# V's loads of the last twenty pairs: 38 rows a band in one, all 144 groups in 3 KB rows in the other

## The chip, the cores and the metric

The kernel runs on one core of a Trainium2 chip. The metric is the device time of one execution in microseconds (us). Engines are named as in the profile: PE (TensorE), DVE (VectorE), ACT (ScalarE), POOL (GpSimd), SP (SyncE); PEld is TensorE's weight load. SP computes nothing here: it issues nearly all transfers, in program order, and stands still at an issue until what that transfer needs is done.

## The reference

Attention in two parts over 8 batches x 8 heads of 576 tokens x 64, then a gated feed-forward layer over all 4,608 tokens.

```python
q_d = q.reshape(B, H, Sd, 4, D).mean(axis=3)      # k_d, v_d the same: 144 groups of four
out_d = sm_attn(q_d, k_d, v_d)                     # full attention over 144 groups
out_up = np.repeat(out_d, 4, axis=2)
mask = np.abs(pos[:, None] - pos[None, :]) < 4     # each token sees 7 neighbours
out_local = softmax(where(mask, scale * q @ k.T, -1e9)) @ v
x = (out_up + out_local)                           # to [B*S, H*D]
out = (np.maximum(x @ w_gate, 0) * (x @ w_val)) @ w_out
```

## The kernel before

**Pairs and slots.** Two heads of a batch make a pair; there are 32. The work is written out by hand, one `slot(n)` after another (L635), for n from -2 to 33; within a slot each engine's instructions have the order in which the code lists them, and a pair passes through several slots. For the last twenty pairs (`p >= NPE`, that is p >= 12) the steps are: loads of Q and K (L161) five or six slots ahead, the loads of V (`load_v` L186, `load_v4` L215) four slots ahead, the casts to 16 bits three and two slots ahead, the DMA transpose of Q and K (`turn_qk` L262) two ahead, the group sums of Q and K on POOL (`pool_qk` L316) one ahead, scores and softmax in the pair's own slot, the DMA transposes of the weights (`turn_a` L487) one after, and the output matmuls (`outputs` L511) and `add_x` two after. The first twelve pairs use TensorE in place of those transposes.

**SP's order in a slot** for these pairs: `turn_a(n-1)` (transposes of `en` and `ad`), `turn_qk(n+2)` (two transposes), the loads of Q and K, `load_v(n+4)` (two loads), `load_v4(n+4)` (one load), then the stores of finished output rows.

**V comes twice.** `load_v` brings overlapping windows of 32 tokens for the local attention: two bands of 48 partitions (0 to 47 and 64 to 111) of `vst`, 18 windows each. A row of a window is one packet of 64 floats, 256 B. The local matmul (L518) reads rows 0 to 37 of a band. `load_v4` brings the first 128 of the 144 groups of each head, four tokens (1 KB) a row, one group a partition; POOL adds the four tokens in two steps (`sum_v4` L221) into `s4`. The last 16 groups come from `v16` by four small matmuls (L377, `v_ps`), with `pool_sb` as weights. `copy_vd` (L418) puts both into `vd`.

**The coarse weights.** `weights_d` (L468) multiplies the exponentials `ed` [80, 4, 144] by the reciprocal sums on POOL into `ad`: 128 keys in blocks 0 to 3, and 16 keys of each in block 4. The transpose then gives `adt` with five blocks of 80, and L535 multiplies them with `vd`: four matmuls over 128 rows, four over 64.

**Feed-forward.** `ffn_do` emits pieces of the feed-forward layer on TensorE between the attention steps, four or five a slot in the slots of the last twenty pairs. What is left when all pairs are through runs at the end.

Of the kernel before, what the change touches and what calls it, by code (L numbers as in the profile page):

```python
# [10 lines left out]
FP32 = mybir.dt.float32  # L11
FP16 = mybir.dt.float16
AF = mybir.ActivationFunctionType
ALU = mybir.AluOpType
# [3 lines left out]
VR = 112  # L18
# [23 lines left out]
def _dap(t_ap: bass.AP, extra_off: int, dims) -> bass.AP:  # L42
    return bass.AP(tensor=t_ap.tensor, offset=t_ap.offset + extra_off, ap=list(dims))
# [3 lines left out]
def kernel(  # L47
# [10 lines left out]
    nc = tc.nc  # L58
    B, H, S, D = q.shape
# [10 lines left out]
    NW = S // 32  # L70
    NPE = 12
# [16 lines left out]
    def pool(name, bufs):  # L88
        return ctx.enter_context(tc.tile_pool(name=name, bufs=bufs))
# [3 lines left out]
    NQK, NA, NV = 4, 2, 3  # L93
    cpool = pool("kept", 1)
    qk_t = [cpool.tile([128, KW], FP16, name=f"qkT{i}") for i in range(NQK)]
    v_t = [cpool.tile([VR, NW, D], FP32, name=f"vst{i}") for i in range(NV)]
    en_t = [cpool.tile([96, 12, 64], FP16, name=f"en{i}") for i in range(NA)]
    ad_t = [cpool.tile([80, 6, 128], FP16, name=f"adn{i}")[:, 0:5] for i in range(NA)]
    p_nat = pool("nat", 4)
    p_v4 = pool("v4", 3)  # L100
    p_16 = pool("h16", 3)
    p_at = pool("at", 2)
    p_adt = pool("adt", 2)
# [15 lines left out]
    p_t1 = pool("t1", 1)  # L119
    p_qkd = pool("qkd", 2)  # L120
    p_sm = pool("sm", 1)
    p_e = pool("e", 2)
    p_st = pool("st", 4)
    p_ed = pool("ed", 2)
    p_vd = pool("vd", 4)
    p_s4 = pool("s4", 3)
    p_od = pool("od", 2)
    psum = ctx.enter_context(tc.tile_pool(name="psum", bufs=6, space=bass.MemoryType.PSUM))
    psum_d = ctx.enter_context(tc.tile_pool(name="psum_d", bufs=2, space=bass.MemoryType.PSUM))

# [5 lines left out]
        nc.gpsimd.memset(t[:, KO + S :], 0.0)  # L136
    for t in en_t + ad_t:
        nc.vector.memset(t, 0.0)

    def bank(shape, name, dt=FP32):  # L140
        return psum.tile(shape, dt, name=name, tag="bank")
# [17 lines left out]
    st = {}  # L159
# [26 lines left out]
    def load_v(p):  # L186
        off = 2 * p * S * D
        vst = v_t[p % NV]

        def win(rows, lo, par, w, nw):  # L190
            nc.sync.dma_start(
                vst[64 * par + lo : 64 * par + lo + rows, w : w + nw, :],
                _dap(
                    v,
                    off + (32 * (2 * w + par) - 3 + lo) * D,
                    [[D, rows], [64 * D, nw], [1, D]],
                ),
            )


        if p == 0:
            win(48, 0, 0, 1, NW - 1)
            win(45, 3, 0, 0, 1)
        else:
            win(48, 0, 0, 0, NW)
        if p == NP - 1:
            win(48, 0, 1, 0, NW - 1)
            nc.vector.memset(vst[96:VR, NW - 1, :], 0.0)
            win(35, 0, 1, NW - 1, 1)
        else:  # L210
            win(48, 0, 1, 0, NW)
        st[p]["vst"] = vst


    def load_v4(p):  # L215
        st[p]["v4"] = v4 = p_v4.tile([128, 2, 4 * D], FP32, name="v4", tag="v4")
        nc.sync.dma_start(
            v4, _dap(v, 2 * p * S * D, [[4 * D, 128], [S * D, 2], [1, 4 * D]])
        )

    def sum_v4(p):  # L221
        s = st[p]
        v4 = s.pop("v4")
        s2 = v4[:, :, 0 : 2 * D]
        nc.gpsimd.tensor_tensor(out=s2, in0=s2, in1=v4[:, :, 2 * D : 4 * D], op=ALU.add)
        s["s4"] = p_s4.tile([128, 2, D], FP32, name="s4", tag="s4")
        nc.gpsimd.tensor_tensor(
            out=s["s4"], in0=s2[:, :, 0:D], in1=s2[:, :, D : 2 * D], op=ALU.add
        )
# [129 lines left out]
                )  # L359

    def pool_v(p):
        s = st[p]
        v16 = s["v16"]
        s["vp"] = vp = bank([128, 4, D], "v_ps")
        v2 = v16.rearrange("p (h l) d -> p h l d", h=2)

        for l in range(8) if p < NPE else ():
            nc.tensor.matmul(
                out=vp[:, 0:2, :],
                lhsT=pool_sb[:, 128 - 16 * l : 256 - 16 * l],  # L370
                rhs=v2[:, :, l, :],
                start=(l == 0),
                stop=(l == 7),
            )
        for c in range(2):
            for h in range(2):
                nc.tensor.matmul(  # L377
                    out=vp[64 * h : 64 * h + 64, 2 + c, :],
                    lhsT=pool_sb[:, 128 - 32 * c : 192 - 32 * c],
                    rhs=v2[:, h, 8, :],  # L380
                    start=True,
                    stop=True,
                )
# [34 lines left out]
    def copy_vd(p):  # L418
        s = st[p]
        s["vd"] = p_vd.tile([128, 4, D], FP16, name="vd", tag="vd")  # L420
        vp = s.pop("vp")
        if p < NPE:
            nc.scalar.copy(out=s["vd"], in_=vp)
        else:
            nc.scalar.copy(out=s["vd"][:, 2:4], in_=vp[:, 2:4])
            nc.scalar.activation(
                out=s["vd"][:, 0:2], in_=s.pop("s4"), func=AF.Copy, scale=0.25
            )

    def exp_d(p, h):  # L430
# [37 lines left out]
    def weights_d(p):  # L468
        s = st[p]
        rd = p_st.tile([80, 4], FP32, name="rd", tag="rd")  # L470
        nc.vector.reciprocal(out=rd, in_=s.pop("sd"))
        ad = s["ad"] = ad_t[p % NA]
        ed = s.pop("ed")
        for o, i, n in (
            (ad[:, 0:4], ed[:, :, 0:128], 128),
            (ad[:, 4].rearrange("p (i t) -> p i t", i=4)[:, :, 0:16], ed[:, :, 128:144], 16),
        ):
            nc.gpsimd.tensor_tensor(  # L478
                out=o, in0=i, in1=rd[:, :, None].to_broadcast([80, 4, n]), op=ALU.mult
            )  # L480

    def adt_tile(p):
        t = p_adt.tile([128, 512], FP16, name="adt", tag="adt")
        st[p]["adt"] = t[:, 0:400].rearrange("p (a b) -> p a b", b=80)
        return st[p]["adt"]

    def turn_a(p):  # L487
# [23 lines left out]
    def outputs(p):  # L511
        s = st[p]
        at, adt, vd, v16 = s["at"], s["adt"], s["vd"], s["v16"]
        s["up"] = up = [bank([128, 9, 32], "u_ps") for _ in range(2)]
        for l in range(9):
            for par in range(2):
                for h in range(2):
                    nc.tensor.matmul(  # L518
                        out=up[par][64 * h : 64 * h + 64, l, :],
                        lhsT=v16[64 * par : 64 * par + 38, 9 * h + l, :],  # L520
                        rhs=at[
                            64 * par : 64 * par + 38,
                            3 * h + l // 3,
                            32 * (l % 3) : 32 * (l % 3) + 32,
                        ],
                        start=True,
                        stop=True,
                    )
        op = bank([128, S // 4], "o_ps")
        for tail in range(2):  # L530
            for c in range(2):
                lo, n, skip = (0, 80, 0) if c == 0 else (80, 64, 16)
                for h in range(2):
                    rows = slice(64 * h, 64 * h + 64) if tail else slice(0, 128)
                    nc.tensor.matmul(  # L535
                        out=op[64 * h : 64 * h + 64, lo : lo + n],
                        lhsT=vd[rows, 2 + c if tail else h, :],
                        rhs=adt[rows, 4 if tail else 2 * h + c, skip : skip + n],
                        start=(tail == 0 and c == 0),
                        stop=(tail == 1 and c == 1),  # L540
                    )
        s["od"] = p_od.tile([128, S // 4], FP32, name="od", tag="od")
        nc.scalar.copy(out=s["od"], in_=op)  # L543
# [91 lines left out]
    def slot(n):  # L635
# [3 lines left out]
        while loaded[0] < min(NP, n + (5 if n < NPE - 2 else 6)):  # L639
            load(loaded[0])  # L640
            if loaded[0] < NPE:
                load_v(loaded[0])
            loaded[0] += 1
        at_stage(n + 4, load_v, load_v4, pe=False)
        store_y()
        at_stage(n, scores, scores_d)
        at_stage(n - 1, turn_en_pe, pe=True)
        at_stage(n, pool_v, mask_l, shift_l, copy_vd, exp_l, max_d)
        if n == 0:
            cast_qk_act(1)  # L650
# [10 lines left out]
        at_stage(n - 1, turn_ad_pe, pe=True)  # L661
        at_stage(n, lambda p: exp_d(p, 0))
        at_stage(n - 1, outputs, pe=True)
        at_stage(n - 2, outputs, pe=False)
        at_stage(n, sums, weights_l)
        at_stage(n - 1, x_stage, pe=True)
# [6 lines left out]
        if n + 2 >= NPP:  # L673
            at_stage(n + 2, cast_v, pe=True)
        at_stage(n + 1, pool_qk, pe=True)
        at_stage(n, weights_d)
        at_stage(n + 3, cast_qk_act, cast_qk_pool, pe=False)
        at_stage(n + 2, cast_v, sum_v4, pe=False)
        if 1 <= n < 5:
            load_h_weights(n - 1)  # L680
# [45 lines left out]
```

## Time and profile before

| | us |
|---|---|
| median of 3 runs | 408.92 |
| lowest and highest | 406.75, 412.8 |
| profiled execution | 405.34 |
| its span, first to last instruction | 403.5 |
| PE busy in the span | 375.6 |
| DVE, ACT, POOL busy | 253.2, 210.4, 191.5 |

Matmuls are pipelined and their ends are modelled, so a busy PE is not a PE at its peak; the start of one group to the start of the next is the better measure. In 117.76 to 273.58 us (slots 13 to 27) POOL is busy for 93.36 of 155.82 us and DVE for 112.11. POOL's instructions of that stage, per pair (line, tile, shapes, count, busy us and mean ns; from the groups kept apart by shape):

```profile
L478 POOL TENSOR_TENSOR adn<-ed,rd 80x512 f16<-80x512 f16 x16 | 16.6, 1037 | 37.4 <-ACT h L247 19.2 <-DVE rd L471 11.0 <-ACT r L576 7.2
...
L225 POOL TENSOR_TENSOR v<-v 128x256 f32<-128x256 f32 x16 | 11.6, 723 | 0.0
...
L227 POOL TENSOR_TENSOR s<-v 128x128 f32<-128x128 f32 x16 | 7.3, 454 | 1.3
L478 POOL TENSOR_TENSOR adn<-ed,rd 80x64 f16<-80x64 f16 x16 | 4.6, 290 | 0.0
```

The last numbers of a line are the idle time of the engine before these instructions and what ended it.

### The profile page before, as it was taken

What the parts mean: (1) busy time and instruction counts of PE and PEld (TensorE: products, weight loads), DVE (VectorE), ACT (ScalarE), POOL (GpSimd) and SP (SyncE); (2) the same over time, 40 slices, a digit from 0 to 9 for tenths busy, and PEclk for the clock granted to TensorE, in tenths of its full rate; (3) what the DMA queues carried; (4) which work ended last, traced back from release to release, by engine and by line L of the source; (5) the groups of instructions that cost most, each with busy time, mean ns of one, the idle gap of its engine ahead of it and who ended that gap; (6) DMA issues with size and microseconds to landing.
All of it is one profiled execution on the core that took longest, in us unless ns stands there. A gap on an engine that the chain in (4) does not pass through costs nothing.

```text
span 403.5 us, 11622 instructions
## 1 busy us (share of the span) xinstructions
PE 375.6 (93%) x4544; PEld 196.4 (49%) x4544; DVE 253.2 (63%) x639; ACT 210.4 (52%) x600; POOL 191.5 (47%) x252
## 2 busy tenths in 40 slices
PE   2699998898999999999999998999699999999996
PEld 2587555454544444444445444444244444444442
DVE  2798699887878767675767675777557432222220
ACT  3577678775757545564545555555345322332321
POOL 5587778764778666666555565544551100000000
PEclk9999999999999999999999999999899999999999
DMA  7999999998999999999999899898831100100012
GB/s 192 229 210 224 232 231 211 233 177 200 213 221 203 178 178 203 204 192 193 198 213 200 191 191 197 184 165 182 168 108 53 51 28 26 54 26 28 37 41 105
DMA packets 172700, 64.24 MB, mean 159 GB/s; under 512 B 150166, under 2 KB 168038, under 8 KB 172646
## 3 DMA queue, kind: packets, MB, share of 16 engines
q1 hardware_dynamic: 166470, 58.63, 69.8%
q0 software_dynamic: 5824, 4.72, 7.7%
q8 instruction: 35, 0.57, 0.6%
q10 hardware_dynamic: 352, 0.16, 0.2%
q14 instruction: 19, 0.16, 0.1%
HBM read 47.87 MB, written 9.44 MB: 142 GB/s over the span
## 4 chain that ended last, share of the span: by engine, by line
PE 77%; ACT 7%; DVE 6%; DMA 4%; issue 3%; POOL 2%; SPq 1%; ACTq 0%; POOLq 0%
PE h_ps L568 42%; PE y_ps L584 23%; PE o_ps L535 2%; PE s_ps L336 2%; ACT ed L437 2%; PE u_ps L518 2%; PE d_ps L353 2%; DVE sm L411 2%; DMA nat<-in_k_dram 1%; PE t_ps L283 1%; DVE s_ps L388 1%; DVE mx L410 1%; PE t_ps L304 1%; PE v_ps L377 1%; ACT r L576 1%
## 5 line engine op out<-in xcount | busy, mean ns | idle before, releaser
L578 DVE TENSOR_TENSOR g<-r,h_ps 128x512 f16<-128x512 f16 x108 | 73.9, 684 | 97.2 <-PE h_ps L568 88.2
L568 PE MATMUL h_ps<-xT,wg_sb 128*128 128x512 f16 x432 | 113.1, 384 | 3.0 <-DVE xT L552 3.0
L568 PE MATMUL h_ps<-xT,wv_sb 128*128 128x512 f16 x432 | 112.4, 383 | 0.0
L584 PE MATMUL y_ps<-wo_sb,g 128*128 128x512 f16 x432 | 98.6, 379 | 0.0
L576 ACT ACTIVATE r<-h_ps 128x512 f16<-128x512 f32 x108 | 64.4, 596 | 46.9 <-PE h_ps L568 46.4
L478 POOL TENSOR_TENSOR adn<-ed,rd 80x512 f16<-80x512 f16 x64 | 41.2, 663 | 67.1 <-ACT r L576 22.8
L568 PEld LDWEIGHTS <-wv_sb 128*128 128x128 f16 x432 | 42.6, 99 | 55.4 <-issue 5.5
L584 PEld LDWEIGHTS <-g 128*128 128x128 f16 x432 | 41.6, 98 | 49.2
L568 PEld LDWEIGHTS <-wg_sb 128*128 128x128 f16 x432 | 38.9, 99 | 43.6 <-issue 1.9
L592 ACT COPY y_sb<-y_ps 128x512 f32<-128x512 f32 x36 | 21.1, 586 | 68.9 <-PE y_ps L584 57.6
L323 POOL TENSOR_TENSOR t<-qkT 128x576 f32<-128x576 f16 x27 | 30.9, 1145 | 39.6 <-DMA qkT<-h 32.7
L437 ACT ACTIVATE ed<-d_ps,nb 80x144 f16<-80x144 f32 x128 | 47.6, 383 | 0.0
L260 POOL CAST v<-vst 112x1152 f16<-112x1152 f32 x32 | 36.7, 1147 | 8.3 <-DMA vst<-in_v_dram 5.3
L449 ACT ACTIVATE e<-sm 96x456 f16<-96x456 f32 x32 | 18.6, 583 | 35.9 <-DVE sm L411 35.8
L249 POOL CAST h<-nat 96x768 f16<-96x768 f32 x35 | 29.7, 849 | 5.6 <-DMA nat<-in_k_dram 3.0
L388 DVE TENSOR_TENSOR s_ps<-s_ps,mask_sb 96x228 f32<-96x228 f32 x64 | 22.2, 390 | 16.0 <-PE s_ps L336 14.0
L552 DVE TENSOR_TENSOR xT<-u_ps,od 128x288 f16<-128x288 f32 x64 | 26.0, 446 | 5.0 <-ACT od L543 5.0
L394 DVE TENSOR_REDUCE d_ps<-d_ps 80x2 f32<-80x288 f32 x64 | 28.9, 452 | 0.0
L247 ACT CAST h<-nat 96x768 f16<-96x768 f32 x29 | 24.3, 841 | 4.3 <-DMA nat<-in_k_dram 4.3
L411 DVE TENSOR_TENSOR sm<-s_ps,mx 96x228 f32<-96x228 f32 x64 | 25.1, 392 | 2.2
L437 ACT ACTIVATION_READ_ACCUMULATOR ed<-d_ps,nb 80x1 f32 x128 | 26.4, 206 | 0.0
L461 DVE TENSOR_TENSOR en<-e,rl 96x456 f16<-96x456 f16 x32 | 23.9, 747 | 1.1
(54 smaller groups left out, 363.5 us busy)
## 6 DMA issues: line engine op xcount, KB each, us to landing
vst<-in_v_dram SPq DMA_DIRECT2D x62, 216.0 KB, 5.2
out_dram<-y_sb SPq DMA_DIRECT2D x36, 256.0 KB, 3.4
nat<-in_q_dram SPq DMA_DIRECT2D x20, 288.0 KB, 3.5
nat<-in_k_dram SPq DMA_DIRECT2D x20, 288.0 KB, 4.3
v<-in_v_dram SPq DMA_DIRECT2D x20, 256.0 KB, 4.8
nat<-in_q_dram SPq DMA_DIRECT2D x12, 192.0 KB, 7.8
nat<-in_k_dram SPq DMA_DIRECT2D x12, 192.0 KB, 5.3
wg_sb<-in_moe_w_gate_dram POOLq DMA_DIRECT2D x4, 384.0 KB, 8.4
```

What stands on the lines that cost most here:

```text
L249: nc.gpsimd.tensor_copy(out=dst, in_=src)
L260: nc.gpsimd.tensor_copy(out=s["v16"], in_=s.pop("vst"))
L323: nc.gpsimd.tensor_tensor(out=t1, in0=qkv[:, :, :, 0], in1=qkv[:, :, :, 1], op=ALU.add)
L388: nc.vector.tensor_tensor(out=sp, in0=sp, in1=mask_sb, op=ALU.add)
L394: nc.vector.tensor_reduce(out=nbr, in_=s["dp"][h], axis=AX.X, op=ALU.max)
L411: nc.vector.tensor_tensor(out=sm[:, half, :], in0=sp, in1=mx[:, half, None].to_broadcast([96, 6, 38]), op=ALU.subtract,)
L437: nc.scalar.activation(out=s["ed"][:, i, :], in_=s["dp"][h][:, c, :], func=AF.Exp, scale=SCALE / 16.0, bias=s["nb"][:, i : i + 1], accum_o ...
L478: nc.gpsimd.tensor_tensor(out=o, in0=i, in1=rd[:, :, None].to_broadcast([80, 4, n]), op=ALU.mult)
L568: nc.tensor.matmul(out=h, lhsT=w[:, kk, bass.ts(jj, 128)], rhs=xT[:, kk, bass.ts(c, TCH)], start=(kk == 0), stop=(kk == 3),)
L576: nc.scalar.activation(out=r, in_=h1, func=AF.Relu)
L578: nc.vector.tensor_tensor(out=g, in0=r, in1=h2, op=ALU.mult)
L584: nc.tensor.matmul(out=y, lhsT=gts[c][jj][:, bass.ts(ty, 128)], rhs=wo_sb[:, jj, :], start=(jj == 0), stop=(jj == NJJ - 1),)
```

## The change

It concerns the pairs from 12 on. `load_v` brings 38 rows of a band in place of 48. `load_v4` brings all 144 groups of a head, as 48 rows of 3 KB (three groups a partition), one load for each head, into partitions 0 to 47 and 64 to 111 of a tile that is kept; POOL sums them all. `pool_v` does nothing for these pairs, and `copy_vd` is one instruction. The coarse weights go into six blocks of 48 keys (key 3j + c at row j of block c), so `adt` has six blocks of 80 and the output takes twelve matmuls over 48 rows. To make room, `e`, `od`, `s4` and `vd` have one buffer less each. The kept V tiles are cleared in rows 32 to 63 at the start.

```diff
-    ad_t = [cpool.tile([80, 6, 128], FP16, name=f"adn{i}")[:, 0:5] for i in range(NA)]
+    ad_t = [cpool.tile([80, 6, 128], FP16, name=f"adn{i}") for i in range(NA)]
+    v4_t = [cpool.tile([VR, 3, 4 * D], FP32, name=f"v4_{i}") for i in range(NV)]
-    p_v4 = pool("v4", 3)
...
-    p_e = pool("e", 2)
+    p_e = pool("e", 1)
-    p_vd = pool("vd", 4)
-    p_s4 = pool("s4", 3)
-    p_od = pool("od", 2)
+    p_vd = pool("vd", 3)
+    p_s4 = pool("s4", 2)
+    p_od = pool("od", 1)
...
+    for t in v4_t:
+        nc.vector.memset(t[32:64], 0.0)
...
+        rows = 48 if p < NPE else 38
         if p == 0:
             win(48, 0, 0, 1, NW - 1)
             win(45, 3, 0, 0, 1)
         else:
-            win(48, 0, 0, 0, NW)
+            win(rows, 0, 0, 0, NW)
         if p == NP - 1:
-            win(48, 0, 1, 0, NW - 1)
+            win(rows, 0, 1, 0, NW - 1)
             nc.vector.memset(vst[96:VR, NW - 1, :], 0.0)
             win(35, 0, 1, NW - 1, 1)
         else:
-            win(48, 0, 1, 0, NW)
+            win(rows, 0, 1, 0, NW)
...
     def load_v4(p):
-        st[p]["v4"] = v4 = p_v4.tile([128, 2, 4 * D], FP32, name="v4", tag="v4")
-        nc.sync.dma_start(
-            v4, _dap(v, 2 * p * S * D, [[4 * D, 128], [S * D, 2], [1, 4 * D]])
-        )
+        st[p]["v4"] = v4 = v4_t[p % NV]
+        for h in range(2):
+            nc.sync.dma_start(
+                v4[64 * h : 64 * h + 48],
+                _dap(v, (2 * p + h) * S * D, [[12 * D, 48], [4 * D, 3], [1, 4 * D]]),
+            )
...
-        s["s4"] = p_s4.tile([128, 2, D], FP32, name="s4", tag="s4")
+        s["s4"] = p_s4.tile([VR, 3, D], FP32, name="s4", tag="s4")
...
     def pool_v(p):
+        if p >= NPE:
+            return
...
-            nc.scalar.copy(out=s["vd"][:, 2:4], in_=vp[:, 2:4])
             nc.scalar.activation(
-                out=s["vd"][:, 0:2], in_=s.pop("s4"), func=AF.Copy, scale=0.25
+                out=s["vd"][0:VR, 0:3], in_=s.pop("s4"), func=AF.Copy, scale=0.25
             )
...
+            a6 = ad.rearrange("p (q c) (h j) -> p h q c j", c=3, h=2)
+            e6 = ed.rearrange("p (h q) (j c) -> p h q c j", h=2, c=3)
+            for h in range(2):
+                nc.gpsimd.tensor_tensor(
+                    out=a6[:, h, :, :, 0:48],
+                    in0=e6[:, h],
+                    in1=rd[:, 2 * h : 2 * h + 2, None, None].to_broadcast([80, 2, 3, 48]),
+                    op=ALU.mult,
+                )
...
-        st[p]["adt"] = t[:, 0:400].rearrange("p (a b) -> p a b", b=80)
+        n = 5 if p < NPE else 6
+        st[p]["adt"] = t[:, 0 : 80 * n].rearrange("p (a b) -> p a b", b=80)
...
-        for tail in range(2):
+        last = 1 if p < NPE else 2
+        for part in range(last + 1):
             for c in range(2):
                 lo, n, skip = (0, 80, 0) if c == 0 else (80, 64, 16)
                 for h in range(2):
-                    rows = slice(64 * h, 64 * h + 64) if tail else slice(0, 128)
+                    if p >= NPE:
+                        rows, iv, ia = slice(64 * h, 64 * h + 48), part, 3 * c + part
+                    elif part:
+                        rows, iv, ia = slice(64 * h, 64 * h + 64), 2 + c, 4
+                    else:
+                        rows, iv, ia = slice(0, 128), h, 2 * h + c
```

More of the change, by code (lines that the diff above doesn't have):

```diff
@@ L365, in pool_v @@
         v2 = v16.rearrange("p (h l) d -> p h l d", h=2)
-        for l in range(8) if p < NPE else ():
+        for l in range(8):
             nc.tensor.matmul(
@@ L420, in copy_vd @@
         s["vd"] = p_vd.tile([128, 4, D], FP16, name="vd", tag="vd")
-        vp = s.pop("vp")
         if p < NPE:
-            nc.scalar.copy(out=s["vd"], in_=vp)
+            nc.scalar.copy(out=s["vd"], in_=s.pop("vp"))
         else:
-            nc.scalar.copy(out=s["vd"][:, 2:4], in_=vp[:, 2:4])
             nc.scalar.activation(
-                out=s["vd"][:, 0:2], in_=s.pop("s4"), func=AF.Copy, scale=0.25
+                out=s["vd"][0:VR, 0:3], in_=s.pop("s4"), func=AF.Copy, scale=0.25
             )
@@ L473, in weights_d @@
         ed = s.pop("ed")
[L474 to L480, printed above, removed]
+        if p < NPE:
+            for o, i, n in (
+                (ad[:, 0:4], ed[:, :, 0:128], 128),
+                (ad[:, 4].rearrange("p (i t) -> p i t", i=4)[:, :, 0:16], ed[:, :, 128:144], 16),
+            ):
+                nc.gpsimd.tensor_tensor(
+                    out=o, in0=i, in1=rd[:, :, None].to_broadcast([80, 4, n]), op=ALU.mult
+                )
[3 more added lines that the diff above has]
+            for h in range(2):
+                nc.gpsimd.tensor_tensor(
+                    out=a6[:, h, :, :, 0:48],
+                    in0=e6[:, h],
+                    in1=rd[:, 2 * h : 2 * h + 2, None, None].to_broadcast([80, 2, 3, 48]),
+                    op=ALU.mult,
+                )
     def adt_tile(p):
         t = p_adt.tile([128, 512], FP16, name="adt", tag="adt")
-        st[p]["adt"] = t[:, 0:400].rearrange("p (a b) -> p a b", b=80)
+        n = 5 if p < NPE else 6
+        st[p]["adt"] = t[:, 0 : 80 * n].rearrange("p (a b) -> p a b", b=80)
         return st[p]["adt"]
@@ L533, in outputs @@
                 for h in range(2):
-                    rows = slice(64 * h, 64 * h + 64) if tail else slice(0, 128)
+                    if p >= NPE:
+                        rows, iv, ia = slice(64 * h, 64 * h + 48), part, 3 * c + part
+                    elif part:
+                        rows, iv, ia = slice(64 * h, 64 * h + 64), 2 + c, 4
+                    else:
+                        rows, iv, ia = slice(0, 128), h, 2 * h + c
                     nc.tensor.matmul(
                         out=op[64 * h : 64 * h + 64, lo : lo + n],
[L537 to L540, printed above, removed]
+                        lhsT=vd[rows, iv, :],
+                        rhs=adt[rows, ia, skip : skip + n],
+                        start=(part == 0 and c == 0),
+                        stop=(part == last and c == 1),
                     )
```

## The prediction

> **What bounds the kernel now.** I read the page's slices first, then the DMA issues of the stretch 117 to 281 us (slots 13 to 27, the middle of the last twenty pairs), then TensorE and SyncE in order of time. TensorE is busy in nearly every slice at nearly full clock, and the DMA engines are just as full until slice 30:
>
> ```profile
> PE   2699998898999999999999998999699999999996
> PEclk9999999999999999999999999999899999999999
> DMA  7999999998999999999999899898831100100012
> ```
>
> So two resources are at their limit together. TensorE in order of time tells which waits. From slot 13 (score matmuls at 117.76) to slot 28 (273.58) its slots follow each other at 155.8 / 15 = 10.39 us, and it stands still for a DMA at two places only, at 242 and again at 285.0 (0.90 us, for `at`):
>
> ```profile
> 242.76 0.46 PE L518 MATMUL u_ps<-at,v 38*64 38x32 f16 x36 [0.70 <-DMA at<-en]
> 243.68 0.44 PE L535 MATMUL o_ps<-adt,vd 128*64 128x80 f16 x8 [0.46 <-DMA adt<-adn]
> ```
>
> SyncE's queue, one slot of it (start, us, line, what is issued):
>
> ```profile
> 249.51 1.28 SPq L490 DMA_TRANSPOSE at<-en  x1
> 250.89 1.20 SPq L491 DMA_TRANSPOSE adt<-adn  x1
> 252.18 2.54 SPq L267 DMA_TRANSPOSE qkT<-h  x2
> 254.78 0.57 SPq L180 DMA_DIRECT2D nat<-in_q_dram  x1
> 255.40 0.59 SPq L180 DMA_DIRECT2D nat<-in_k_dram  x1
> 256.08 1.75 SPq L191 DMA_DIRECT2D vst<-in_v_dram  x2
> 257.94 2.17 SPq L217 DMA_DIRECT2D v<-in_v_dram  x1
> 260.14 0.47 SPq L598 DMA_DIRECT2D out_dram<-y_sb  x1
> 260.72 1.30 SPq L490 DMA_TRANSPOSE at<-en  x1
> ```
>
> It issues without a pause; its slots (first `at` transpose 117.20, sixteenth 281.17) take 164.0 / 15 = 10.93 us. An unhindered pair of L191 loads took 0.98 us at 12 us; here it takes 1.75, since the engines' queues are full. TensorE is thus faster than the transfers by 0.5 us a slot; it begins level with SyncE and is 8.5 us ahead at slot 24, and then the transfers hold it. Both are within 5% of binding: little is to be gained, much to be lost, in the transfers.
>
> ```profile
> q1 hardware_dynamic: 100428, 31.26, 96.6%
> ...
> vst<-in_v_dram SPq DMA_DIRECT2D x29, 216.0 KB, 5.0
> ...
> vst<-in_v_dram SPq DMA_DIRECT2D x1, 204.0 KB, 4.3
> vst<-in_v_dram SPq DMA_DIRECT2D x1, 8.8 KB
> ```
>
> The first row is packets, MB and share of 16 engines in that stretch; the others are V's loads with the time to landing. The last has none: this is the 35-row load of the last pair. A landing is read from sixteen marks on the load's semaphore, and this load left eight: one 0.55 us after the issue, before data could land, and seven after 2.2 to 2.8 us. The 45-row load of the first pair left one mark 0.7 us after its issue and fifteen later ones. Loads of 48 rows leave sixteen, the one of 17 windows (204 KB) too. So rows are dealt in equal shares: 48 = 16 x 3, 45 = 15 x 3, 35 = 7 x 5. The number of engines is the largest up to 16 that divides the rows; the count of windows plays no part.
>
> **The change part by part.** *V's window loads, 48 to 38 rows.* 38 = 2 x 19. By the rows above such a load goes to two engines: 38 x 18 = 684 packets of 256 B, 342 on each, where now 864 / 16 = 54 are on each. No row shows which engines; I take the same two for both loads of a pair and for every pair, since nothing in the trace tells of a turn. The Trainium skill (DMA: Bandwidth & Descriptors, "Why a DMA increments its semaphore by 16 and not by 1") gives the rule: the engine count is the largest number up to 16 that divides the slowest dimension of both sides, and SyncE's loads use the lowest-numbered ones; the marks above agree with the first half, the second no run here shows.
>
> Price of a packet: in 117 to 281 us the trace has 91,322 packets of 256 B, median 18 ns, mean 22.3. In 70 to 90 us, where the 256 B packets on SyncE's queue are those of V and of the last pairs' first Q and K loads, they average 19.5. With fourteen engines mostly idle, contention should be nearer the lower values: I take 19.5, with 18 and 22.3 as ends. So V's windows cost each of the two engines 684 x 19.5 ns = 13.3 us a slot. Their share of everything else, a slot: other 256 B packets (91,322 - 25,907 of V) / 15 / 16 = 273 x 19.5 = 5.3 us; eight 2 KB packets of the store x 84 ns = 0.7; six 3 KB rows of the new V load, estimated at 1.5 of the 2 KB ones, 126 ns, = 0.8; small ones 0.1. Together 6.9. The slot of those two engines is 20.2 us against TensorE's 10.39, so nothing of TensorE can hide it.
>
> SyncE issues the other transfers in 249.51 to 256.08 and on, some 8 us a slot without the V windows. A load lands 5.0 us after issue though its own 54 packets need 1.2, so about 4 us of work stands in an engine's queue; when a V load has been let through, that stock and the following 6.9 us cover these 8 us. If the queue were shallow, SyncE's 8.2 us would add to the V time instead of lying beside it: that is the upper end. The wait sits at L191 in SyncE's order; behind it stand the other V load, the store and the next slot's transposes `at`, `adt`, `qkT`, and for those wait TensorE (L518, L535) and GpSimd (L323, already 30.0 us on `qkT` in this stretch). Cast, scores and output of a pair are one to three slots apart, some 20 us or more, so latency alone does not add; the rate does.
>
> The sum. Slot 8's V load is issued at 76.0; the twenty loads are in slots 8 to 27. V: 20 x 13.34 = 266.8. The rest on the same engines: slots 13 to 27, 15 x 6.9 = 103.5; slots 10 to 12 without `at` and `adt`, 3 x 5.7, and 2.8 for one more pair of Q and K loads, = 19.9; slot 9, 3.6. SyncE starts slot 28 at 76.0 + 393.8 = 469.8, now 281.2: 188.6 us later. What follows hangs on slot 28's transposes (TensorE's wait at 285.0 is for them) and has the same instructions in the same order: span 403.5 + 188.6 = 592, and 1.8 us lie around the span (405.34 against 403.5): 594.
>
> *V's second load.* 256 packets of 1 KB (mean 72.8 ns, 18.6 us of engine time a slot) become 96 rows of 3 KB (12.1): minus 0.4 us a slot over 16 engines. One more issue on SyncE: between 0.40 (L217 at 280.16, queue empty) and 0.70 us, in the 8.2 above; 48 rows go to 16 engines. All of it is counted in the 6.9.
>
> *GpSimd.* The sums: 256 elements took 723 ns, 128 took 454, so 2.1 ns an element over 185; 384 and 192 give 991 and 588: plus 0.40 us a pair. The weights: 512 and 64 elements took 1037 and 290, 1327 together; two of 288 give 2 x 664 = 1328 by the same line. The new read steps over three elements; the nearest row, L323, steps over two and fits the line (576 elements, 1146), so I take nothing, with half as much again (0.7 us) as upper end. GpSimd is busy 93.4 of 155.8 us in slots 13 to 27, 6.2 a slot; 7.3 at worst, still under TensorE's slot.
>
> *ScalarE.* The 267 ns copy goes, the 314 ns one grows by 64 elements (some 60 ns): minus 0.2 us, hidden, since L449 behind it waits for VectorE anyway.
>
> *TensorE.* The four `v_ps` matmuls go: 0.19 us from start to start. Eight `o_ps` matmuls in 0.37 us become twelve with 48 rows: 0.13 us at the pace of `u_ps` (36 in 0.40), 0.55 at today's: minus 0.24 to plus 0.18. In sum minus 0.43 to 0 a slot, off the path while the transfers bind.
>
> *adt* grows from five blocks to six, 96 packets or 0.1 us an engine, counted. The three new VectorE clears (768 elements, about 0.75 us each by the 378 ns of the 384-element ones) end some 2.3 us later, at about 5 us; VectorE's first real work is at 10.5. The fewer buffers of `e`, `od`, `s4`, `vd` cost nothing: each next writer already waits, through `sm` or through ScalarE's order, for something behind the last reader.
>
> **The rivals.** *All engines share the 38 rows* (three rows each to thirteen, or finer). Transfers then fall by 360 x 22.3 + 6.5 us - 1.7 us = 12.8 engine us a slot, 0.8 on each of 16: 10.93 becomes 10.1, under TensorE's 10.39. The waits of 2.1 us go, TensorE's part gives 0 to 8.6: 393 to 401, with the 1.8 around it 395 to 403, likeliest 401, not slower. It decides as soon as an engine gets no more than about 54 + 25 packets of a load, for then TensorE has the longer slot. For it: nothing in the change asks for fewer engines. Against it: 35 rows went to seven engines and not to twelve. *Two engines, but others for each load.* Over 16 engines the work is that of the first rival and a load lands in 342 x 19.5 = 6.7 us plus the queue, well inside its two slots: about 402. Nothing in the trace speaks for it. *One engine:* 1368 x 19.5 = 26.7 us a slot; 20 x 26.7 + 127 = 661, slot 28 at 737, total about 861. The divisor 2 speaks against it.
>
> **How the numbers follow.** Forecast 0.88; all engines 0.05; changing engines 0.02; one engine 0.03; slower by another cause, such as GpSimd's new steps, 0.02. The time is the forecast's 594. Low end: 18 ns throughout, V 246.2, the rest 117, slot 28 at 439, total 563. High end: 22.3 ns and SyncE's issues added, V 305 and 146, slot 28 at 527, total 651; contention on two busy engines may add some, so 560 to 665, which leaves out the rivals (0.12) and a little of the tails. This kernel's runs spread over 406.75 to 412.8, so 2% is about what a measurement tells from no change. The profiled execution (405.34) is 0.9% under their median of 408.92; beside 190 us that is nothing. Faster 0.02 and same 0.05 come from the first two rivals, slower 0.93 from the others.
>
> **What would show it.** Right: V's window loads land after more than 8 us instead of 5.0; the L191 issues of a slot take over 8 us instead of 1.75; the DMA digits of the stage fall to about 4 while the stage lasts some 190 us longer; TensorE waits for `at`, GpSimd for `qkT`; far fewer marks a V load. Wrong: landings still near 5 us and DMA digits of 9; then the dealing is not by divisor. If landings are long but TensorE does not wait, the engines differ from load to load. If GpSimd's weights come out well over 1.33 us a pair, the step has a price that I left at nothing.

## The result, and the profile after

| | us |
|---|---|
| changed kernel, median of 4 runs (553.77 to 561.09) | 558.62 |
| kernel before, median of 4 runs (406.75 to 412.8) | 408.53 |
| ratio, 95% interval | 1.3639 (1.3492 to 1.3785) |
| profiled execution and its span | 556.9, 555.1 |

Medians are over all executions of a kernel; ratios leave out those more than 1.5% above its fastest.

The changed kernel is slower by 36%, in the direction that was forecast and through the two engines that were forecast, but 35 us faster than the number: 558.6 lies just under the low end of 560. The slices of the changed kernel (40 of 13.9 us each):

```profile
PE   2899989876274676658557766856586499999997
PEclk9999989997676886887788588868878799999999
DMA  9999985644465447545734654564455642010102
```

From slice 8 to slice 32 neither TensorE nor the transfers are full, where before both were: in slots 13 to 27 the packets take 0.54 of the sixteen engines' time, before 0.98, and TensorE waits. One slot of SyncE's queue (start, us, line, what is issued), and TensorE in the same slot:

```profile
286.48 1.23 SPq L508 DMA_TRANSPOSE at<-en  x1
287.82 1.20 SPq L509 DMA_TRANSPOSE adt<-adn  x1
289.11 2.55 SPq L272 DMA_TRANSPOSE qkT<-h  x2
291.71 1.11 SPq L182 DMA_DIRECT2D nat<-in_q_dram  x1
292.88 0.59 SPq L182 DMA_DIRECT2D nat<-in_k_dram  x1
293.56 5.95 SPq L193 DMA_DIRECT2D vst<-in_v_dram  x2
299.60 5.22 SPq L221 DMA_DIRECT2D v<-in_v_dram  x2
304.87 0.89 SPq L622 DMA_DIRECT2D out_dram<-y_sb  x2
305.87 1.24 SPq L508 DMA_TRANSPOSE at<-en  x1
```

```profile
289.58 0.67 PE L536 MATMUL u_ps<-at,v 38*64 38x32 f16 x36 [6.83 <-DMA at<-en]
```

SyncE's slot is 19.4 us here; over slots 13 to 27 it is (435.93 - 153.04) / 15 = 18.86 us, against 10.93 before. The 8 us more are at the window loads (L193) and at what follows them (L221). In the whole span TensorE waits 97.7 us for `at` (1.6 before) and GpSimd 151.9 us for `qkT`; the first line is of the kernel before, the others of the changed one:

```profile
POOL t L323 <- DMA qkT<-h: 32.7, 14, 5.7
...
POOL t L328 <- DMA qkT<-h: 151.9, 15, 13.7
...
PE u_ps L536 <- DMA at<-en: 97.7, 15, 9.1
```

The issue table has no landing time any more, neither for the V windows nor for SyncE's other transfers, which count on the same semaphores in turn:

```profile
vst<-in_v_dram SPq DMA_DIRECT2D x39, 171.0 KB
```

The marks on the semaphores tell more: each of the thirty 38-row loads of slots 13 to 27 leaves three, one early (0.6 to 1.7 us after the issue of a pair's first load; for the second, when SyncE has been let through) and two late, when data has landed: two engines. The first load of a pair lands 7.6 us after its issue and the second 12.0 (medians); before it was 5.0.

### The profile page after: what moved, and what is told of

The parts are those of the page before. It is cut to its first block, busy times and chain, and to the rows that moved or that the text cites. A ratio compares the mean times of both kernels' runs of the same rounds, so it can differ in the third digit from the quotient of the medians.

```text
span 555.1 us, 11678 instructions
## 1 busy us (share of the span) xinstructions
PE 412.6 (74%) x4544; PEld 207.2 (37%) x4544; DVE 258.7 (47%) x642; ACT 209.1 (38%) x580; POOL 199.1 (36%) x252
## 4 chain that ended last, share of the span: by engine, by line
PE 37%; SPq 17%; DMA 13%; POOL 12%; DVE 9%; ACT 6%; issue 5%; POOLq 0%; ACTq 0%; DVEq 0%
PE h_ps L592 21%; PE y_ps L608 11%; SPq L221 10%; DMA qkT<-h 3%; DMA at<-en 3%; DMA out_dram<-y_sb 3%; POOL adn L492 3%; POOL v L265 2%; SPq L272 2%; POOL v L230 2%; POOL h L254 2%; DVE sm L417 2%; DMA nat<-in_q_dram 2%; DVE s_ps L394 2%; ACT ed L441 2%
## 5 line engine op out<-in xcount | busy, mean ns | idle before, releaser
L592 PE MATMUL h_ps<-xT,wg_sb 128*128 128x512 f16 x432 | 127.6, 422 | 1.3 <-DVE xT L576 1.1
L592 PE MATMUL h_ps<-xT,wv_sb 128*128 128x512 f16 x432 | 123.3, 412 | 7.0 <-ACT y_sb L616 7.0
L328 POOL TENSOR_TENSOR t<-qkT 128x576 f32<-128x576 f16 x27 | 31.4, 1162 | 226.1 <-DMA qkT<-h 151.9
L608 PE MATMUL y_ps<-wo_sb,g 128*128 128x512 f16 x432 | 108.2, 406 | 0.0
L536 PE MATMUL u_ps<-at,v 38*64 38x32 f16 x1152 | 19.7, 200 | 100.6 <-DMA at<-en 97.7
L592 PEld LDWEIGHTS <-wv_sb 128*128 128x128 f16 x432 | 45.7, 106 | 70.6 <-issue 27.0
L608 PEld LDWEIGHTS <-g 128*128 128x128 f16 x432 | 44.4, 104 | 58.0 <-issue 15.1
L592 PEld LDWEIGHTS <-wg_sb 128*128 128x128 f16 x432 | 41.5, 105 | 51.8 <-issue 14.1
L536 PEld LDWEIGHTS <-v 38*64 38x64 f16 x1152 | 16.4, 133 | 111.7 <-DMA at<-en 104.8
L453 ACT ACTIVATE e<-sm 96x456 f16<-96x456 f32 x32 | 18.6, 581 | 59.5 <-DVE sm L417 59.5
L492 POOL TENSOR_TENSOR adn<-ed,rd 80x288 f16<-80x288 f16 x40 | 25.8, 666 | 14.4 <-issue 14.4
L567 ACT COPY od<-o_ps 128x144 f32<-128x144 f32 x32 | 9.0, 280 | 47.2 <-PE o_ps L559 47.1
```

Source lines behind the costliest of these rows:

```text
L328: nc.gpsimd.tensor_tensor(out=t1, in0=qkv[:, :, :, 0], in1=qkv[:, :, :, 1], op=ALU.add)
L492: nc.gpsimd.tensor_tensor(out=a6[:, h, :, :, 0:48], in0=e6[:, h], in1=rd[:, 2 * h : 2 * h + 2, None, None].to_broadcast([80, 2, 3, 48]), o ...
L536: nc.tensor.matmul(out=up[par][64 * h : 64 * h + 64, l, :], lhsT=v16[64 * par : 64 * par + 38, 9 * h + l, :], rhs=at[64 * par : 64 * par + 38,
L592: nc.tensor.matmul(out=h, lhsT=w[:, kk, bass.ts(jj, 128)], rhs=xT[:, kk, bass.ts(c, TCH)], start=(kk == 0), stop=(kk == 3),)
L608: nc.tensor.matmul(out=y, lhsT=gts[c][jj][:, bass.ts(ty, 128)], rhs=wo_sb[:, jj, :], start=(jj == 0), stop=(jj == NJJ - 1),)
```

## The experiments

Theory A: a load's rows are dealt to the largest number of engines up to 16 that divides them. Theory B: the new 3 KB load in two issues is at fault, for the chain of waits names L221 as SyncE's costliest line. Theory C: any row count that is no multiple of 16 falls to few engines. "Before" in the tables below is the kernel before, run beside.

**48 rows in the changed kernel.**

```diff
-        rows = 48 if p < NPE else 38
+        rows = 48
```

> The changed kernel with 48 rows a band again, all else as changed. Theory A (a load's rows go to the largest number of engines up to 16 that divides them, so 38 rows go to two, and this alone makes the loss): V's window loads are on sixteen engines again, SyncE's L193 pair takes 1 to 2 us a slot instead of 5.7, L221 under 1.5 instead of 5.2, and the time is 398 to 406 us: transfers 0.3 us a slot under those before, TensorE 0 to 0.4 us a slot less. Theory B (the new 3 KB load in two issues is what SyncE stands at: 5.2 us a slot at L221, the costliest SyncE line of the chain of waits): L221 stays near 5 us a slot and the time stays above 480 us.

**38 rows in the kernel before.**

```diff
+        rows = 48 if p < NPE else 38
...
-            win(48, 0, 0, 0, NW)
+            win(rows, 0, 0, 0, NW)      # the other band the same
```

> The kernel before with 38 rows a band for the last twenty pairs, and nothing else of the change. Theory A: V's windows on two engines, the next issue behind them (the old single V load, L218) stands about 5 us, slots of 18 to 19.5 us, time 545 to 575 us. Theory B: the old V load is unchanged, so the time is 400 to 410 us.

**39 and 41 rows in the changed kernel.**

```diff
-        rows = 48 if p < NPE else 38
+        rows = 48 if p < NPE else 39      # and 41
```

> The changed kernel with 39 rows a band instead of 38. 39 = 3 x 13. Theory A: thirteen engines with three rows each, 54 packets an engine as with 48 rows, time 398 to 408 us. Theory C (any number of rows that is no multiple of 16 falls to very few engines): 540 to 580 us, as with 38. Theory B: as with 38.

> The changed kernel with 41 rows a band instead of 38. 41 is a prime. Theory A: one engine, 41 x 18 = 738 packets a load, 1,476 a slot on it; at 15 to 18 ns a packet 22 to 27 us a slot plus 7 to 8 for the rest, 29 to 35 a slot in place of 18.9, twenty slots: 760 to 880 us. Theory C: about the time of 38 rows, 550 to 600 us.

| rows a band | engines by A | us | slot, us | marks a load |
|---|---|---|---|---|
| 48 (e1) | 16 | 414.87; ratio 1.0145 (1.0059 to 1.0232) | 11.56 | 16 |
| 39 (e3) | 13 | 416.25, one run | 11.45 | 14 (two loads: 12, 13) |
| 38 (after) | 2 | 558.62 | 18.86 | 3 |
| 38, else before (e2) | 2 | 554.04, one run | 18.67 | |
| 41 (e4) | 1 | 781.21, one run | 30.17 | 2 |

Theory A alone stands. With 48 rows nearly the whole loss is gone; 38 rows in the kernel before make all of it but about 1%, so the 3 KB loads have at most that part in it (B); and 39 rows, no multiple of 16 either, cost nothing clear beside 48, while 41 rows cost far more than 38 (C). The marks agree with the dealing: with 39 rows one early mark and thirteen later ones, with 41 one and one. The times of e2 and with 41 rows came out in their ranges; 48 rows missed theirs (398 to 406) by 9 us and 39 rows theirs (398 to 408) by 8, which is taken up below. With 48 rows the L193 issues take 2.3 us a slot on average, where 1 to 2 were expected, and L221, which had seemed the costly line, 1.2; in one slot:

```profile
220.00 3.78 SPq L193 DMA_DIRECT2D vst<-in_v_dram  x2
223.88 1.13 SPq L221 DMA_DIRECT2D v<-in_v_dram  x2
```

and with 41, where the first of the two window loads has passed before the first line:

```profile
398.50 10.43 SPq L193 DMA_DIRECT2D vst<-in_v_dram  x1
409.03 10.72 SPq L221 DMA_DIRECT2D v<-in_v_dram  x2
```

SyncE does not stand at the load that is slow. The first window load passes in half a microsecond. The second is let through about 2 us before the first one's last mark (in the slot above at 299.51, the mark is at 301.46; with 41 rows at 439.24 and 441.1), as if the first had to be handed to its engines before; and the next transfer, whatever it is, when the same holds for the second. So half of the wait appears at the innocent line behind.

**The 3 KB loads ahead of the window loads.**

```diff
-        at_stage(n + 4, load_v, load_v4, pe=False)
+        at_stage(n + 4, load_v4, load_v, pe=False)
```

> The changed kernel (38 rows) with the 3 KB loads issued before the window loads in each slot. If the 5.2 us that SyncE stands at L221 belong to the window loads in front of it, they move to what now follows these loads (the store or the transposes of the next slot), L221 falls under 1.5 us and the time stays 550 to 562 us. If they belong to the 3 KB loads, they stay at L221.

568.46 us (one run), 10 us over the changed kernel's median and above the range; why it is slower stays open. The wait moved as expected: L221 is down to 1.42 us here and the store behind the window loads stands for 4.80.

```profile
300.23 1.42 SPq L221 DMA_DIRECT2D v<-in_v_dram  x2
301.69 5.78 SPq L193 DMA_DIRECT2D vst<-in_v_dram  x2
307.52 4.80 SPq L622 DMA_DIRECT2D out_dram<-y_sb  x1
```

**The second band's load on ScalarE's queue.**

```diff
-            nc.sync.dma_start(
+            (nc.scalar if par and p >= NPE else nc.sync).dma_start(
...
-        at_stage(n + 4, load_v, load_v4, pe=False)
+        at_stage(n + 4, lambda p: load_v(p, (0,)), load_v4, pe=False)
...
+        at_stage(n + 4, lambda p: load_v(p, (1,)), pe=False)      # behind exp_d(p, 1)
```

> The changed kernel (38 rows), with the second band's load issued from ScalarE's queue, late in the slot, in place of SyncE's. If both loads of a pair go to the same two engines whatever queue issues them, those engines still have 684 packets a slot (9.8 us at the 14.3 ns that 38 and 41 rows together give) and their share of the rest (6 to 7 us): at least 16 us a slot, time 500 to 560 us. If the second load goes to other engines, SyncE stands only for 342 packets (4.9 us less a slot, about 14 us a slot): 445 to 470 us.

551.04 us (one run), slots of 17.76 us. Two queues do not help: the same two engines serve both loads. From the marks, ScalarE's load issued at 257.8 lands 9.1 us later, SyncE's issued at 260.7 after 12.1 us, 6.0 us behind the first. The Trainium skill (DMA: Bandwidth & Descriptors, "Why a DMA increments its semaphore by 16 and not by 1") says that SyncE's and ScalarE's loads use the lowest-numbered engines. This run agrees in so far as both queues' loads share their engines, by 551 us where other engines would have given 445 to 470; which engines they are, no run here shows.

**Q and K on ScalarE's queue.**

```diff
             for i, src in ((0, q), (1, k)):
-                nc.sync.dma_start(
+                nc.scalar.dma_start(
```

> The changed kernel (38 rows), with the last twenty pairs' Q and K loads issued from ScalarE's queue in place of SyncE's (1.8 us of SyncE's slot). Serial theory (a slot is SyncE's standing at the V loads plus its 8 us of other issues, the two engines run dry meanwhile): the slot falls by about 1.8 us to 17 us, time 515 to 535 us. Engine theory (the two engines are never idle, 684 x 17.5 ns + 6.9 us a slot, as the prediction had it in form): unchanged, 550 to 562 us.

527.43 us (one run), slots of 17.09 us: 1.77 us less, about what these two issues had taken of SyncE (1.80). The serial theory stands: SyncE's other issues add to its standing at the V loads, and the work on the two engines does not cover them.

**46 rows.**

```diff
-        rows = 48 if p < NPE else 38
+        rows = 48 if p < NPE else 46
```

> The changed kernel with 46 rows a band: 46 = 2 x 23, two engines again, 828 packets a slot on each instead of 684. At 14.3 ns a packet (the slope between 38 and 41 rows) the slot grows by 2.1 us and the time to 594 to 604 us; at the 17.5 ns of the engine theory by 2.5 us, 604 to 611; at the prediction's 19.5 ns by 2.8 us, 611 to 618.

602.54 us (one run), slots of 21.17 us, three marks a load. 144 packets more on each engine cost 2.31 us: 16.0 ns a packet; from 38 to 41 rows, 792 more packets cost 11.31 us: 14.3 ns. The marks give a third value: in slots 13 to 27 of the changed kernel the second load of a pair lands 5.12 us after the first (median), 15.0 ns for each of 342 packets. A fourth is the most direct. In the changed kernel's 290 to 400 us (40 slices of 2.75 us) the transfers fall again and again to 36 GB/s, the stretches in which the window loads alone move:

```profile
DMA  9821169555114896411669551147973116679111
GB/s 107 182 65 36 36 178 244 115 120 115 34 36 111 226 107 150 103 36 36 180 151 107 120 125 39 36 138 194 106 172 80 36 36 172 158 112 206 43 36 36
```

In 298 to 304.5 us these are 922 packets, all of 256 B: 142 a us, on two engines one every 14.1 ns. With 41 rows 638 packets go by in 410 to 419 us, 71 a us, on one engine again one every 14.1 ns; with 46 rows the stretches have 142 a us as well. So 144 packets more are 2.03 us of the 2.31.

**What the rest of the change costs.** With 48 rows the changed kernel should have been some 1 to 3% faster, by the 398 to 406 us expected, and is 1.45% slower (0.6 to 2.3%). The loss shows at TensorE: in the time of SyncE's slots 13 to 27 it stands still for 10.3 us, 8.6 of them for `at`, and its own slots take 11.03 us; in the kernel before it stands still for 1.2 us and its slots take 10.39. Four runs look for the cause.

```diff
-        nc.sync.dma_start(
-            v4, _dap(v, 2 * p * S * D, [[4 * D, 128], [S * D, 2], [1, 4 * D]])
-        )
+        for h in range(2):
+            nc.sync.dma_start(
+                v4[:, h], _dap(v, (2 * p + h) * S * D, [[4 * D, 128], [1, 4 * D]])
+            )
```

> The kernel before (48 rows, old shapes) with its single 256 KB load of V issued as two loads of 128 KB, one a head: same packets, one more issue a slot on SyncE. It asks what makes the changed kernel with 48 rows slower than the one before (415 against 410 us). Issue theory (SyncE's queue has no slack, 10.2 of 10.93 us a slot, so 0.42 us more are paid): 412 to 418 us. Packet theory (the 3 KB rows take 222 ns each, 21.5 us of engine time a slot where the old load took 18.6, and the sixth adt block 1.6 more): unchanged, ratio 0.995 to 1.005.

```diff
-    v4_t = [cpool.tile([VR, 3, 4 * D], FP32, name=f"v4_{i}") for i in range(NV)]
+    v4_t = [cpool.tile([VR, 3, 4 * D + 2], FP32, name=f"v4_{i}")[:, :, 0 : 4 * D] for i in range(NV)]
```

> The changed kernel with 48 rows, and the kept V tile padded by two floats a group, so that a 3 KB row is three packets of 1 KB. Issue theory: nothing changes for SyncE, 412 to 417 us. Packet theory, if it is the long row to one partition that is slow: near the time before, ratio below 1.007; if it is the bytes: 288 x 73 ns = 21 us, as now, 412 to 417 us.

```diff
-            nc.sync.dma_start(      # in load_v4
+            nc.scalar.dma_start(
...
-        at_stage(n + 4, load_v, load_v4, pe=False)
+        at_stage(n + 4, load_v, pe=False)
...
+        at_stage(n + 4, load_v4, pe=False)      # behind exp_d(p, 1)
```

> The changed kernel with 48 rows, and the two 3 KB loads issued from ScalarE's queue in the second half of the slot. Issue theory: SyncE is freed of 1.24 us a slot, 10.3 us, about TensorE's 10.2: 400 to 406 us, faster than before. Packet theory (engines full: 174.8 us of engine time a slot over 16 engines = 10.9): 409 to 416 us.

> The kernel before with its second V load issued from ScalarE's queue in the second half of the slot. Issue theory: SyncE's slot falls from 10.93 by 0.83 us under TensorE's 10.39: 400 to 405 us. Packet theory (168.9 us of engine time over 16 engines = 10.56): 404 to 409 us.

| | median us | ratio to before, 95% interval | SyncE's slot, us | TensorE's |
|---|---|---|---|---|
| before, two issues (f6) | 412.76 | 1.0102 (1.0053 to 1.0151) | 11.08 | 10.54 |
| 48 rows, padded (f7) | 431.57 | 1.0514 (1.0466 to 1.0562) | 12.25 | 11.72 |
| 48 rows, 3 KB loads by ScalarE (f3) | 424.44 | 1.0325 (1.027 to 1.0381) | 10.86 | 11.10 |
| before, second V load by ScalarE (f4) | 417.56 | 1.0162 (1.0108 to 1.0217) | 10.71 | 10.92 |

Slots are read from one profiled execution of each kernel, TensorE's from score matmuls to score matmuls.

One more issue a slot costs 1.0%, and its interval overlaps that of the 48-row version (0.6 to 2.3%): it can be most of that loss, but no run shows that it is. The padded tile is the worst of all, above every range given for it. Its own packets do not account for it: 1 KB pieces take 66.2 ns, 19.5 us of engine time a slot, but the 256 B packets rise from 22.3 to 25.2 ns and take 18 us a slot more. As the padding shifts the rows by 8 B too, this run does not tell which of the two does it.

f3 and f4 went against both theories. SyncE's slots did become shorter, but only after SyncE had come late to the stage, at 132.1 and 129.2 us instead of 117.2. TensorE came to its slot 13 only 2 to 4 us late (121.94 and 119.86 instead of 117.76), and its slots became longer than before. In f4 SyncE stands before the stage for ScalarE's loads (waits of SyncE's queue in 70 to 132 us: total, times, longest):

```profile
SPq L191 <- DMA v<-in_v_dram: 14.2, 3, 8.2
SPq L180 <- DMA v<-in_v_dram: 12.0, 2, 9.8
```

Neither L191 nor L180 uses that data. In the trace SyncE's load is to count on the semaphore on which ScalarE's counts (number 109 at 116.50 and at 119.12 us), and SyncE waits until ScalarE's, issued late in its slot, has landed. So the last two runs leave the early slots as they were.

```diff
-        nc.sync.dma_start(      # in load_v4; its place in the slot as above
+        (nc.scalar if p >= 18 else nc.sync).dma_start(
```

> The kernel before with its second V load issued from ScalarE's queue for pairs 18 to 31 only (slots 14 to 27). If SyncE's issues bind in these slots and the loss of the earlier try was only the standing of SyncE in slots 8 to 12: slots of 10.7 us as there, start of the stage at 117 as before, 402 to 408 us, ratio 0.985 to 0.998. If SyncE's standing for ScalarE's loads comes along to slot 14: 412 to 420 us.

> The changed kernel with 48 rows, its two 3 KB loads issued from ScalarE's queue for pairs 18 to 31 only. If SyncE's extra issue is what the rest of the change loses by: slots of 10.8 us instead of 11.56, 403 to 409 us, ratio to the kernel before 0.985 to 1.0. If the engines' load binds (174.8 us a slot over 16): 411 to 417 us, as without this step.

| | median us | ratio to before, 95% interval | SyncE's slot, us | TensorE's |
|---|---|---|---|---|
| before, from pair 18 on (g1) | 409.71 | 1.0053 (1.002 to 1.0085) | 10.64 | 10.46 |
| 48 rows, from pair 18 on (g2) | 418.80 | 1.0227 (1.0163 to 1.0291) | 11.25 | 11.05 |

Neither came out in the ranges of a theory: g1 lies between the two, g2 above both. SyncE's slots are shorter by 0.3 us in both; TensorE's are not (10.39 and 11.03 without this step), and the times are not. In g1 there was little to win: TensorE stands still for 1.7 us of this stage, in the kernel before for 1.2. The packet theory's sums do not hold either: in g1 the recorded packet times add up to 1.11 times what sixteen engines have, so an engine's recorded packets overlap, and such a sum over 16 is no price of a slot. No version beats the kernel before. How the 1.45% divide between the extra issue, the 3 KB rows, the sixth `adt` block and the buffers that `e`, `od`, `s4` and `vd` gave up, which no run restored, stays open.

## Where the prediction was right, and where it was wrong

The time came out under the stated range. The step that failed is the price of V's windows, 684 packets at 19.5 ns or 13.3 us a slot, with 18 ns as its lowest value: the packets follow each other at 14.1 ns, 9.6 us a slot. A second step failed the other way, the overlap of SyncE's issues with the engines' other work.

**Right: the dealing of the rows.** 38 rows to two engines was read from seven marks of a 35-row load and fifteen of a 45-row load; 38, 39, 41 and 46 rows bear it out. That both loads of a pair use the same engines, a choice that no row then supported, is shown by f1. The three rivals with other dealings fall with it. Without the change of rows none of the loss remains but 1.45%.

**Wrong: the two terms of a slot.** The prediction had 13.3 us for V's windows and 6.9 us of other work on the same engines, 20.2 together. Measured: 18.86.

- *684 packets x 19.5 ns.* A packet costs 14.1 to 16.0 ns by the four measures above, 9.6 to 10.9 us a slot. The 18 ns taken as the low end was the median duration of a packet in the records. In the stretches in which the windows alone move each packet is recorded with 18 ns too, but the next follows after 14.1: the recorded durations overlap, 1.28 packets at a time on an engine. This is the step that put the number too high, and its low end was no lower bound.
- *6.9 us of work that covers SyncE's 8 us.* It did not cover them: f2 shows SyncE's issues added to the time at the V loads, as the prediction had it for its upper end. What is left of 18.86 after V is 7.9 to 9.2 us, near SyncE's 8.2 and above the 6.9.

The second error took back part of the first, so it is in part luck that the number is only 6% off. In the sum: slots 8 to 12 were put at 90.2 us and took 77.3; slots 13 to 27 at 303.6 and took 282.9; what follows at 122.3 and took 119.2. The three differences, 12.9, 20.7 and 3.1 us, are the 37 us between the forecast span of 592 and the measured 555.1.

**Half right: where the wait stands.** It was put at the window loads (L193 now) with over 8 us a slot; 5.6 us are there (median) and 5.2 at L221 behind it, the load that the prediction had down for 0.4 to 0.7 us an issue. The first load of a pair lands after 7.6 us, not more than 8; the second does, after 12.0.

**Right: the compute engines.** GpSimd's lines after:

```profile
L492 POOL TENSOR_TENSOR adn<-ed,rd 80x288 f16<-80x288 f16 x30 | 19.4, 666 | 1.0 <-issue 1.0
...
L230 POOL TENSOR_TENSOR v<-v 112x384 f32<-112x384 f32 x15 | 15.0, 997 | 0.0
...
L232 POOL TENSOR_TENSOR s<-v 112x192 f32<-112x192 f32 x15 | 8.8, 589 | 1.2
```

666, 997 and 589 ns against 664, 991 and 588 from the line through two sizes; the step over three elements costs nothing. ScalarE's 112x192 copy takes 0.36 us, estimated at 0.37. On TensorE twelve `o_ps` matmuls take 0.32 us from their start to the next group's (f3, 203.46 to 203.78), eight took 0.37; inside the bounds.

**Wrong: V's second load, put at 12.1 us of engine time a slot instead of 18.6.** A 3 KB row was estimated at 126 ns from 2 KB ones. In the changed kernel, on half idle engines, its median is 121 and its mean 161; beside full queues, with 48 rows, they are 205 and 222, or 21.5 us of recorded time a slot. So by the records the load became dearer, not cheaper; as recorded durations overlap, they do not say what that costs. The first rival's 395 to 403 us would have been wrong too: its nearest runs, e1 and e3, took 415 and 416. At 36% this is hidden; at 1% the sign of the forecast saving did not come out, from a cause that stays open.

## What to carry to other kernels

Before a row count of a transfer is cut, factor it: what counts is how many engines share the rows, and 38, 41 and 46 rows fall to two, one and two, while 39 rows keep thirteen. A transfer on few engines is recognised by missing landing marks and by the next transfer on the queue standing for microseconds: look one instruction ahead of the line that waits. A packet's recorded duration is not its price on a busy engine; take the price from the spacing of two landings, from two sizes, or from the packets a microsecond in a stretch in which that load alone moves. A shorter slot on the queue is worth nothing while TensorE's slots do not get shorter: read the slots of both.

## What the runs showed of the hardware that was not expected

- On an engine that works off one long load alone, 256 B packets follow each other every 14.1 ns, though each is recorded at 18 (638 packets in 9 us on the one engine with 41 rows).
- Eleven engine microseconds a slot less (39 rows against 48: 163.8 against 174.8 us of packets) change the slot by 0.1 us. The thirteen engines in use have the same 54 packets a load in both; this fits the fullest engine setting the pace, not the mean. It is not shown: SyncE's issues, 10.5 and 10.6 us a slot, may set it as well.
- TensorE's granted clock is lower where it is starved: 0.79 of full speed in 153 to 436 us of the changed kernel and 0.68 in slots 13 to 27 with 41 rows, 1.00 in slots 13 to 27 before. Over the whole execution the 128x512 matmuls with `wg_sb` (L592) show 422 ns on average instead of 384. What this adds to the time no run separates, as TensorE waits there in any case.
